# Zero-filled full-row subtraction product, halves of 288 queries, and earlier maxima in the first batch of an attention and two-MLP kernel

## The chip, the cores and the metric

The kernel runs on one core of a Trainium2 chip. The metric is the time of one execution on the device in microseconds, from the median of repeated runs. A profiled execution has its own time, beside the span from the first to the last instruction in its trace. TensorE multiplies matrices into PSUM, VectorE, ScalarE (ACT) and GpSimd (POOL) work on elements, and the SyncE queue (SP) issues the DMAs.

## The reference

The inputs are `q`, `k` and `v` of 4 batches, 8 heads, 576 positions and 64 dimensions. Scores below the row's maximum less `tau` are dropped before the softmax. The heads' outputs are put side by side to 2304 rows of 512 and go through two MLPs with 2048 hidden columns; the first applies a rational function, the second a clipped square.

```python
scores = scale * np.matmul(q, k.transpose(0, 1, 3, 2))
thresh = np.max(scores, axis=-1, keepdims=True) - tau
scores = np.where(scores >= thresh, scores, -1000000000.0)
attn = np.exp(scores - np.max(scores, axis=-1, keepdims=True))
attn = attn / (np.sum(attn, axis=-1, keepdims=True) + 1e-09)
out = np.matmul(attn, v)
# first MLP
h = x @ w_in
P = a[0] + a[1] * h + a[2] * h2 + a[3] * h3
Q = 1.0 + np.abs(b[0]) * np.abs(h) + np.abs(b[1]) * h2
x = (P / (Q + 1e-06)) @ w_out
# second MLP
h = x @ w_in
x = np.where(h >= 1, h, np.where(h <= -1, 0.0, (h + 1) ** 2 / 4)) @ w_out
```

## The kernel before

The heads of a batch are taken in four pairs (`NP`). A head's 576 positions (`S`) are four tiles of 128 and a tail of 64; the tails of both heads of a pair share one tile, so a pair has nine tiles of columns in the transposed queries and keys `qkT`: four of the first head, the shared tail, four of the second. Queries and keys are split into two 16-bit halves; `kT2` holds the keys with their halves exchanged, so that two products make one score tile.

The first batch is handled apart from the others. Before it there is nothing to lay its work beside, except the first MLP's weights: these come as 64-bit floats, and are converted by VectorE (lines 222 to 224), ACT (240, 211, 202) and POOL (206), while the first batch runs. For each pair, `row_max` (line 495) computes the scores with queries in rows, into one PSUM bank at a time, and reduces each to the row's maximum (`most`, line 508). The maxima are cut into three 16-bit pieces (lines 533 to 537), and a product with the identity lays them into three rows of queries, `mrow` (lines 538 to 543). `transposed` (line 546) then computes the scores with keys in rows: for each tile two score products and a third that subtracts the maximum, with `less16` (three rows with the negated weights of the pieces) as weights and `mrow` as the moving operand (line 560). The 576 queries of a tile go as 512 and 64 columns, since a bank holds 512. ACT takes the exponential (562), VectorE drops what is below the threshold (563), and `sums` (566) multiplies the result by the values in 32 bits, again 512 and 64 columns, into two banks that add up over all tiles of a head. `take` (574) copies a finished head's sums to SBUF, `divide` (581) divides by them.

`first_attention` (597) sets the order. It walks nine tiles for each pair; `held` keeps the sums one tile behind the scores. `row_max` is a generator of three pieces: the maxima of the first head, those of the second, and the rest with `mrow`. The next pair's pieces are called for at steps 1, 4 and 7 of a pair (`n % 3 == 1`), and the pair after that is prepared (`prep_pair`, line 311: six loads, scaling, splitting, a transposing DMA and two copies into `kT2`) at step 4. `qkT` and `kT2` have two buffers each. The calls give priorities; the order in which each engine's instructions stand is worked out by a planner from priorities and its own estimate of times, and each engine then runs its list in order.

After the first batch, 192 steps of the two MLPs follow, with the conversion of the second MLP's weights and the attention of the other three batches laid beside them.

Of the kernel before, what the change touches and what calls it, by code (L numbers as in the profile page):

```python
# [9 lines left out]
F16 = mybir.dt.float16  # L10
F32 = mybir.dt.float32
# [20 lines left out]
N_TEMP, N_POLY, N_WT, N_WH, N_GG, N_ROW, N_SC = 5, 3, 3, 2, 4, 3, 2  # L32
# [7 lines left out]
def tile_attention_moe_moe2(  # L40
# [18 lines left out]
    V, A, G, T, Q = nc.vector, nc.scalar, nc.gpsimd, nc.tensor, nc.sync  # L59
    B, H, S, D = q.shape  # L60
    P = 128
    NP = H // 2
    NT = S // P
    ST = S - NT * P
    C = 2 * NT + 1
# [9 lines left out]
    W = NF * TB  # L75
# [5 lines left out]
    ap = ctx.enter_context(tc.tile_pool(name="ap", bufs=2))  # L81
    xp = ctx.enter_context(tc.tile_pool(name="xp", bufs=1))
    mp = ctx.enter_context(tc.tile_pool(name="mp", bufs=2))
    sp = ctx.enter_context(tc.tile_pool(name="sp", bufs=4))
    dp = ctx.enter_context(tc.tile_pool(name="dp", bufs=1, space=DRAM))
    ps_1 = ctx.enter_context(tc.tile_pool(name="ps_1", bufs=1, space=PSUM))
    ps_2 = ctx.enter_context(tc.tile_pool(name="ps_2", bufs=1, space=PSUM))
# [2 lines left out]
    ident = cp.tile([P, P], F32, name="ident")  # L90
    make_identity(nc, ident)
    fixed = mp.tile([P, 2 * W], F16, name="fixed", tag="gg", bufs=N_GG)
    ident16, less16 = fixed[:, 0:P], fixed[0:3, P : 2 * P]
    V.tensor_copy(ident16, ident)
    less = cp.tile([3, 1], F32, name="less")
    V.tensor_scalar(less, ident[0:3, 0:1], -PIECES[0], None, op0=ALU.mult)
    for n in range(1, 3):
        V.scalar_tensor_tensor(less, ident[0:3, n : n + 1], -PIECES[n], less, op0=ALU.mult, op1=ALU.add)
    V.tensor_copy(less16, less.to_broadcast([3, P]))


    def small(n, name, keep=False):
# [246 lines left out]
    M = NT * P  # L349
# [145 lines left out]
    def row_max(pr, qkT, kT2):  # L495
        k1 = qkT[:, C:, :].rearrange("p c s -> p (c s)")
        k2 = kT2.rearrange("p c s -> p (c s)")
        mx = sp.tile([P, 18], F32, name=f"mx0_{pr}", tag="c2", bufs=3)

        def bank(name):  # L500
            return ps_1.tile([P, 512], F32, name=f"sm{pr}_{name}", tag="ph0")

        def dots(dst, c, cols, k0):
            n = dst.shape[-1]
            T.matmul(dst, qkT[:, c, cols], k1[:, k0 : k0 + n], start=True, stop=False)
            T.matmul(dst, qkT[:, c, cols], k2[:, k0 : k0 + n], start=False, stop=True)

        def most(n, src, m=1):
            V.tensor_reduce(mx[:, n : n + m], src, axis=AX.X, op=ALU.max)

        halves = [slice(i * ST, (i + 1) * ST) for i in range(2)]
        for ab in range(2):
            for t in range(NT):
                s = bank(f"{ab}{t}")
                dots(s, ab * (NT + 1) + t, slice(0, P), ab * (M + P))
                most(ab * NT + t, s)
            yield
        s = bank("t").rearrange("p (n k) -> p n k", n=2 * NT)
        for n in range(2 * NT):
            dots(s[:, n], n + n // NT, slice(0, P), M + n // NT * ST)  # L520
        most(2 * NT + 1, s, 2 * NT)
        s = bank("r")
        for i, r in enumerate(halves):
            dots(s[r], NT, r, i * (M + P))
        most(2 * NT, s)
        s = bank("rt")[:, 0:ST]
        for i, r in enumerate(halves):
            dots(s[r], NT, r, M + i * ST)
        most(4 * NT + 1, s)
        n = 2 * NT + 1  # L530
        m = mx[:, 0:n]
        V.tensor_tensor(m, m, mx[:, n:], op=ALU.max)
        pcs = sp.tile([P, 3, n], F16, name=f"pcs{pr}", tag="ka", bufs=2)
        for x in range(3):
            V.tensor_scalar(pcs[:, x], m, 1.0 / PIECES[x], None, op0=ALU.mult)
            if x < 2:
                V.scalar_tensor_tensor(m, pcs[:, x], -PIECES[x], m, op0=ALU.mult, op1=ALU.add)
        mrow = ap.tile([P, 2 * S], F16, name=f"mrow{pr}", tag="hl", bufs=N_ROW)[0:3]
        for c0, c1 in ((0, NT), (NT, 2 * NT), (2 * NT, n)):
            pm = ps_1.tile([P, 512], F32, name=f"pmr{pr}_{c0}", tag="aux")  # L540
            for c in range(c0, c1):
                T.matmul(pm[0:3, (c - c0) * P : (c - c0 + 1) * P], pcs[:, :, c], ident16, start=True, stop=True)
            A.copy(mrow[:, c0 * P : c1 * P], pm[0:3, 0 : (c1 - c0) * P])
        yield mrow

    def transposed(pr, ab, t, data, n):

        con, qkT, kT2, mrow = data
        name = f"{pr}_{ab}_{t}"
        s = ps_2.tile([P, 1024], F32, name="st" + name, tag="acc" if n % 2 else "s")[:, 0:S]  # L550
        q1 = qkT[:, 0:C, :].rearrange("p c s -> p (c s)")
        tiles = [(ab, slice(0, P), slice(0, P), ab * (NT + 1) + t)]
        if t == NT:
            tiles = [(i, slice(i * ST, (i + 1) * ST), slice(i * ST, (i + 1) * ST), NT) for i in range(2)]
        for i, r, cols, c in tiles:
            for to, k0, m0, w in ((0, i * (M + P), i * M, M), (M, M + i * ST, 2 * M + i * ST, ST)):
                dst = s[r, to : to + w]
                T.matmul(dst, qkT[:, C + c, cols], q1[:, k0 : k0 + w], start=True, stop=False)
                T.matmul(dst, kT2[:, c, cols], q1[:, k0 : k0 + w], start=False, stop=False)
                T.matmul(dst, less16[:, 0 : r.stop - r.start], mrow[:, m0 : m0 + w], start=False, stop=True)  # L560
        e = mp.tile([P, 2 * W], F32, name="et" + name, tag="tp", bufs=N_TEMP)[:, 0:S]
        A.activation(e, s, AF.Exp, scale=con[:, 0:1])
        V.scalar_tensor_tensor(e, s, con[:, 2:3], e, op0=ALU.is_ge, op1=ALU.mult)
        return e

    def sums(pv, ab, pr, t, e, vv, first, last):

        w = vv[pr][:, t, ab : ab + 2] if t < NT else vv[NP][:, pr, ab : ab + 2]
        w = w.rearrange("p x d -> p (x d)")
        r = slice(ab * ST, (ab + 1) * ST) if t == NT else slice(0, P)  # L570
        for dst, c0 in pv:
            T.matmul(dst, w[r], e[r, c0 : c0 + dst.shape[-1]], start=first, stop=last)

    def take(pv, ab, x, d):
        h, o = (slice(i * D, (i + 1) * D) for i in (ab, 1 - ab))
        for src, c0 in pv:
            c = slice(c0, c0 + src.shape[-1])
            A.copy(d[h, c], src[o])
            A.copy(x[h, c], src[h])

    def divide(pr, x, d):
        r = mp.tile([P, 2 * W], F32, name=f"rd0_{pr}", tag="tp", bufs=N_TEMP)[:, 0:S]
# [14 lines left out]
    def first_attention():  # L597

        ahead = [prep_pair(0, 0, False)]
        yield  # L600
        vv = first_v()
        yield
        xT[0] = [xp.tile([P, 2 * KT, TB], F16, name=f"xT0_{j}", tag="xT", bufs=NB) for j in range(NB)]
        ahead.append(prep_pair(0, 1, False))
        yield
        for mrow in row_max(0, *ahead[0][1:]):
            yield
        n = 0
        for pr in range(NP):
            con, qkT, kT2 = ahead.pop(0)  # L610
            data = con, qkT, kT2, mrow
            rows = row_max(pr + 1, *ahead[0][1:]) if ahead else iter(())
            x = ap.tile([P, S], F32, name=f"x0_{pr}", tag="e", bufs=N_SC)
            d = ap.tile([P, S], F32, name=f"d0_{pr}", tag="sc", bufs=N_SC)
            held = []
            for ab, t in [(0, t) for t in range(NT + 1)] + [(1, t) for t in range(NT)]:
                e = transposed(pr, ab, t, data, n)
                for f in held:
                    f()
                if t == 0:  # L620
                    pv = [(ps_1.tile([P, 512], F32, name=f"pv0_{pr}_{ab}", tag="pv"), 0),
                          (ps_1.tile([P, 512], F32, name=f"pt0_{pr}_{ab}", tag="ph1")[:, 0:ST], M)]
                    held = [partial(sums, pv, 1, pr, NT, tail, vv, True, False)] if ab else []
                    held.append(partial(sums, pv, ab, pr, t, e, vv, not ab, False))
                elif t == NT or (ab and t == NT - 1):
                    held = [partial(sums, pv, ab, pr, t, e, vv, False, True), partial(take, pv, ab, x, d)]
                    tail = e
                else:
                    held = [partial(sums, pv, ab, pr, t, e, vv, False, False)]
                if n % 3 == 1:  # L630
                    mrow = next(rows, None)
                if n % 9 == 4 and pr + 2 < NP:
                    ahead.append(prep_pair(0, pr + 2, False))
                n += 1
                yield
            for f in held:
                f()
            divide(pr, x, d)
        yield
# [201 lines left out]
    for n in range(N_FIRST):  # L841
        with at(36 * n / N_FIRST - 40):
            next(att)
        while halves and len(halves) * N_FIRST > 2 * NCH * (N_FIRST - 1 - n):
            with at(2.4 * (2 * NCH - len(halves)) - 40):
                i, x = halves.pop(0)
# [83 lines left out]
```

## Time and profile before

| | us |
|---|---|
| median of 3 runs | 1297.07 |
| lowest and highest of the 3 | 1291.64, 1303.17 |
| the profiled execution's own time | 1302.64 |
| its span | 1300.5 |
| busy in the span: TensorE products | 1121.9 |
| VectorE | 1015.2 |
| ACT | 823.8 |
| POOL | 499.4 |

Busy shares are means over the whole span, whose stages differ; the first batch lies in about the first 224 us of it. Starts of TensorE's products are recorded, their ends are modelled, so that products that follow each other seem to overlap: what one costs is read from start to start. The clock column gives what TensorE was granted of its 2.4 GHz; its lower level is 1.2 GHz, 0.5 in these columns.

### The profile page before, as it was taken

The numbers are of one execution on the slowest core, as the hardware profiler recorded it, in microseconds if no ns is written. First come the engines' busy times: TensorE is split into PE (matmuls) and PEld (weight loads), VectorE is DVE, ScalarE is ACT, GpSimd is POOL, SyncE is SP. The second block draws the span as 40 slices with busy tenths as digits, with TensorE's granted clock in tenths as the row PEclk, the third lists the DMA queues.
The fourth block names the chain that finished last, engine by engine and source line by source line (L and its number), as shares of the span: only waits on it lengthen the run. The fifth ranks groups of instructions, "written<-read, shape, count | busy, mean of one in ns | idle before, by whom it ended". The sixth has DMA issues, their size and how long they took to land.

```text
span 1300.5 us, 31124 instructions
## 1 busy us (share of the span) xinstructions
PE 1121.9 (86%) x12354; PEld 973.5 (75%) x12354; DVE 1015.2 (78%) x2399; ACT 823.8 (63%) x1469; POOL 499.4 (38%) x673
## 2 busy tenths in 40 slices
PE   2689779478784889999889999999789998999998
PEld 1244334378683778889878899898778998999998
DVE  6687654999999887768999776889997677897431
ACT  3466454676766667757777577777765766676332
POOL 2223211553553555531146355422454554122221
PEclk9699677598986999989999999999899999999999
DMA  7644431633377567771379465901794559106100
GB/s 207 197 148 157 143 130 69 234 119 131 131 281 238 116 114 129 146 216 44 87 183 219 88 124 139 245 34 44 182 220 88 105 102 266 46 2 208 53 14 25
DMA packets 220273, 176.34 MB, mean 136 GB/s; under 512 B 181984, under 2 KB 193248, under 8 KB 211936
## 3 DMA queue, kind: packets, MB, share of 16 engines
q1 hardware_dynamic: 220128, 174.36, 50.3%
q8 instruction: 96, 1.57, 0.5%
q14 instruction: 49, 0.40, 0.1%
HBM read 106.83 MB, written 21.50 MB: 99 GB/s over the span
## 4 chain that ended last, share of the span: by engine, by line
PE 33%; DVE 21%; DMA 8%; issue 5%; POOL 4%; ACT 3%; SPq 1%; DVEq 0%; ACTq 0%; POOLq 0%
PE acc L829 14%; PE ph L815 14%; DMA eT<-hl 5%; DVE e L373 2%; PE pv L399 2%; POOL hl L384 2%; DVE sc L411 2%; DVE t L708 2%; DVE t L707 2%; DVE t L709 1%; DVE t L702 1%; DMA rqk<-in_k_dram 1%; DVE t L703 1%; DVE t L704 1%; DVE qk L209 1%
## 5 line engine op out<-in xcount | busy, mean ns | idle before, releaser
L829 PE MATMUL acc<-gg,wc 128*128 128x192 f16 x4608 | 432.7, 249 | 26.8 <-POOL gg L206 12.6
L815 PEld LDWEIGHTS <-wc 128*128 128x128 f16 x4608 | 393.6, 100 | 28.4 <-issue 15.4
L829 PEld LDWEIGHTS <-wc 128*128 128x128 f16 x4608 | 389.1, 99 | 28.8 <-issue 26.8
L206 POOL TENSOR_TENSOR gg<-t,gg 128x384 f16<-128x384 f32 x192 | 190.1, 992 | 447.2 <-ACT gg L202 370.0
L815 PE MATMUL ph<-xT,wc 128*128 128x192 f16 x2304 | 221.1, 254 | 16.5 <-DVE t L704 11.5
L815 PE MATMUL ph<-yT,wc 128*128 128x192 f16 x2304 | 218.8, 249 | 3.3 <-DVE t L762 2.4
L384 POOL TENSOR_TENSOR hl<-e,hl 128x256 f16<-128x256 f32 x216 | 156.1, 744 | 0.0
L202 ACT CAST gg<-t 128x384 f16<-128x384 f32 x192 | 96.9, 507 | 71.0 <-DVE t L762 33.1
L761 DVE SCALAR_TENSOR_TENSOR t<-t,c 128x384 f32<-128x384 f32 x96 | 64.8, 675 | 70.9 <-ACT t L760 70.8
L373 DVE SCALAR_TENSOR_TENSOR e<-sc,nt,e 128x576 f32<-128x576 f32 x108 | 93.3, 865 | 31.8 <-ACT e L372 31.1
L206 POOL TENSOR_TENSOR wc<-wt,wc 128x256 f16<-128x256 f32 x64 | 46.7, 763 | 143.3 <-ACT wc L202 143.3
L372 ACT ACTIVATE e<-sc,nt,con 128x576 f32<-128x576 f32 x108 | 93.5, 866 | 10.6 <-POOL hl L384 3.7
L760 ACT ACTIVATE t<-ph,c 128x384 f32<-128x384 f32 x96 | 64.0, 667 | 50.6 <-PE ph L815 50.3
L399 PE MATMUL pv<-v,eT 128*128 128x65 f16 (+3 forms) x1680 | 71.7, 196 | 23.5 <-DMA eT<-hl 23.3
L381 ACT CAST hl<-e 128x576 f16<-128x576 f32 x108 | 72.2, 668 | 30.0 <-DVE e L373 29.2
L700 ACT ACTIVATE t<-ph,sc 128x384 f32<-128x384 f32 x96 | 55.4, 577 | 54.9 <-PE ph L815 54.8
L399 PEld LDWEIGHTS <-eT 128*128 128x128 f16 (+1 forms) x1680 | 64.4, 102 | 32.6 <-DMA eT<-hl 29.4
L382 POOL TENSOR_TENSOR hl<-e,hl 128x64 f16<-128x64 f32 x108 | 39.4, 365 | 128.2 <-ACT hl L381 125.8
L411 DVE TENSOR_SCALAR_CACHE_REDUCE sc<-s 128x576 f32<-128x576 f32 x108 | 80.8, 748 | 9.4 <-PE s L366 8.9
L705 ACT ACTIVATE t<-t,lc 128x384 f32<-128x384 f32 x96 | 67.9, 707 | 18.3 <-DVE t L702 18.0
L365 PE MATMUL s<-qkT 128*128 128x512 f16 (+1 forms) x240 | 64.3, 295 | 14.7 <-DVE sc L411 12.1
L412 ACT ACTIVATE nt<-mx,ln_e,con 128x1 f32<-128x1 f32 x108 | 41.6, 385 | 54.3 <-DVE sc L411 53.7
(218 smaller groups left out, 1891.8 us busy)
## 6 DMA issues: line engine op xcount, KB each, us to landing
wc<-scratch SPq DMA_DIRECT2D x56, 1024.0 KB, 5.7
rw<-in_moe_w_in_dram SPq DMA_DIRECT2D x16, 1024.0 KB, 5.4
rw<-in_moe_w_out_dram SPq DMA_DIRECT2D x16, 1024.0 KB, 5.1
scratch<-wc SPq DMA_DIRECT2D x8, 1024.0 KB, 4.0
scratch<-wh SPq DMA_DIRECT2D x16, 512.0 KB, 2.8
kT<-qkT SPq DMA_DIRECT2D x32, 144.0 KB, 2.4
rqk<-in_q_dram SPq DMA_DIRECT2D x16, 256.0 KB, 3.1
rqk<-in_k_dram SPq DMA_DIRECT2D x16, 256.0 KB, 3.0
```

The source lines that it names most:

```text
L202: A.copy(hi, src)
L206: G.tensor_tensor(lo[:, p], src[:, p], hi[:, p], op=ALU.subtract)
L372: A.activation(e, s, AF.Exp, bias=nb, scale=con[:, 0:1])
L373: V.scalar_tensor_tensor(e, s, th, e, op0=ALU.is_ge, op1=ALU.mult)
L381: A.copy(hi, e)
L384: G.tensor_tensor(lo_w[:, p], e[:, whole][:, p], hi[:, whole][:, p], op=ALU.subtract)
L399: T.matmul(pv[rows, 0:w], eT[:, c, cols], vv[:, h * NT + x if x < NT else H * NT + h, at : at + w], start=(n == 0), stop=(n == len(blocks) ...
L411: V.tensor_scalar(s, banks[:, 0:S], 1.0, -LARGEST, op0=ALU.mult, op1=ALU.max, accum_out=mx)
L705: A.activation(r, u, AF.Ln, bias=lc[:, 1:2], scale=lc[:, 0:1])
L761: V.scalar_tensor_tensor(u, u, top, u, op0=ALU.min, op1=ALU.mult)
L815: last = T.matmul(ph[:, f, :], w[:, wx, kt, f * P : (f + 1) * P], rhs, start=(n == 0), stop=(n == 3 * KT - 1))
L829: T.matmul(dst, w[:, wx, f, d * P : (d + 1) * P], gg[:, gx, f, :], start=(i == 0 and f == 0 and n == 0 and d % 2 == 0), stop=(i == NCH - 1 ...
```

## The change

The subtraction's weights get 128 rows, with zeros from row 3 on, and `mrow` becomes a tile of 128 rows that POOL fills with zeros before ACT writes the first three. The maxima are numbered in the order of the columns of `qkT` (first head, tail, second head), so that the queries of a head are one run of 576 columns; it is cut into two halves of 288, each in a bank of its own, for the scores and for the sums. `take` copies the halves; for the second head, whose tail comes first, the second half of `take` has three pieces. The reduction of the eight tail products is made in two. The three pieces of the next pair's maxima are called for at steps 0, 2 and 4 of a pair, the preparation of the pair after that at step 5.

```diff
@@ -90,13 +90,14 @@
     ident = cp.tile([P, P], F32, name="ident")
     make_identity(nc, ident)
     fixed = mp.tile([P, 2 * W], F16, name="fixed", tag="gg", bufs=N_GG)
-    ident16, less16 = fixed[:, 0:P], fixed[0:3, P : 2 * P]
+    ident16, less16 = fixed[:, 0:P], fixed[:, P : 2 * P]
     V.tensor_copy(ident16, ident)
     less = cp.tile([3, 1], F32, name="less")
     V.tensor_scalar(less, ident[0:3, 0:1], -PIECES[0], None, op0=ALU.mult)
     for n in range(1, 3):
         V.scalar_tensor_tensor(less, ident[0:3, n : n + 1], -PIECES[n], less, op0=ALU.mult, op1=ALU.add)
-    V.tensor_copy(less16, less.to_broadcast([3, P]))
+    G.memset(less16, 0.0)
+    V.tensor_copy(less16[0:3], less.to_broadcast([3, P]))
 
 
     def small(n, name, keep=False):
@@ -513,20 +514,21 @@
             for t in range(NT):
                 s = bank(f"{ab}{t}")
                 dots(s, ab * (NT + 1) + t, slice(0, P), ab * (M + P))
-                most(ab * NT + t, s)
+                most(ab * (NT + 1) + t, s)
             yield
         s = bank("t").rearrange("p (n k) -> p n k", n=2 * NT)
         for n in range(2 * NT):
             dots(s[:, n], n + n // NT, slice(0, P), M + n // NT * ST)
-        most(2 * NT + 1, s, 2 * NT)
+        for ab in range(2):
+            most(2 * NT + 1 + ab * (NT + 1), s[:, ab * NT : (ab + 1) * NT], NT)
         s = bank("r")
         for i, r in enumerate(halves):
             dots(s[r], NT, r, i * (M + P))
-        most(2 * NT, s)
+        most(NT, s)
         s = bank("rt")[:, 0:ST]
         for i, r in enumerate(halves):
             dots(s[r], NT, r, M + i * ST)
-        most(4 * NT + 1, s)
+        most(3 * NT + 1, s)
         n = 2 * NT + 1
         m = mx[:, 0:n]
         V.tensor_tensor(m, m, mx[:, n:], op=ALU.max)
@@ -535,30 +537,32 @@
             V.tensor_scalar(pcs[:, x], m, 1.0 / PIECES[x], None, op0=ALU.mult)
             if x < 2:
                 V.scalar_tensor_tensor(m, pcs[:, x], -PIECES[x], m, op0=ALU.mult, op1=ALU.add)
-        mrow = ap.tile([P, 2 * S], F16, name=f"mrow{pr}", tag="hl", bufs=N_ROW)[0:3]
+        mrow = ap.tile([P, 2 * S], F16, name=f"mrow{pr}", tag="hl", bufs=N_ROW)
+        G.memset(mrow, 0.0)
         for c0, c1 in ((0, NT), (NT, 2 * NT), (2 * NT, n)):
             pm = ps_1.tile([P, 512], F32, name=f"pmr{pr}_{c0}", tag="aux")
             for c in range(c0, c1):
                 T.matmul(pm[0:3, (c - c0) * P : (c - c0 + 1) * P], pcs[:, :, c], ident16, start=True, stop=True)
-            A.copy(mrow[:, c0 * P : c1 * P], pm[0:3, 0 : (c1 - c0) * P])
+            A.copy(mrow[0:3, c0 * P : c1 * P], pm[0:3, 0 : (c1 - c0) * P])
         yield mrow
 
     def transposed(pr, ab, t, data, n):
 
         con, qkT, kT2, mrow = data
         name = f"{pr}_{ab}_{t}"
-        s = ps_2.tile([P, 1024], F32, name="st" + name, tag="acc" if n % 2 else "s")[:, 0:S]
+        s = ps_2.tile([P, 1024], F32, name="st" + name, tag="acc" if n % 2 else "s")
+        s = s.rearrange("p (z n) -> p z n", z=2)[:, :, 0 : S // 2]
         q1 = qkT[:, 0:C, :].rearrange("p c s -> p (c s)")
         tiles = [(ab, slice(0, P), slice(0, P), ab * (NT + 1) + t)]
         if t == NT:
             tiles = [(i, slice(i * ST, (i + 1) * ST), slice(i * ST, (i + 1) * ST), NT) for i in range(2)]
         for i, r, cols, c in tiles:
-            for to, k0, m0, w in ((0, i * (M + P), i * M, M), (M, M + i * ST, 2 * M + i * ST, ST)):
-                dst = s[r, to : to + w]
-                T.matmul(dst, qkT[:, C + c, cols], q1[:, k0 : k0 + w], start=True, stop=False)
-                T.matmul(dst, kT2[:, c, cols], q1[:, k0 : k0 + w], start=False, stop=False)
-                T.matmul(dst, less16[:, 0 : r.stop - r.start], mrow[:, m0 : m0 + w], start=False, stop=True)
-        e = mp.tile([P, 2 * W], F32, name="et" + name, tag="tp", bufs=N_TEMP)[:, 0:S]
+            for z in range(2):
+                dst, of = s[r, z], slice(i * S + z * S // 2, i * S + (z + 1) * S // 2)
+                T.matmul(dst, qkT[:, C + c, cols], q1[:, of], start=True, stop=False)
+                T.matmul(dst, kT2[:, c, cols], q1[:, of], start=False, stop=False)
+                T.matmul(dst, less16[:, 0 : r.stop - r.start], mrow[:, of], start=False, stop=True)
+        e = mp.tile([P, 2 * W], F32, name="et" + name, tag="tp", bufs=N_TEMP)[:, 0:S].rearrange("p (z n) -> p z n", z=2)
         A.activation(e, s, AF.Exp, scale=con[:, 0:1])
         V.scalar_tensor_tensor(e, s, con[:, 2:3], e, op0=ALU.is_ge, op1=ALU.mult)
         return e
@@ -568,15 +572,16 @@
         w = vv[pr][:, t, ab : ab + 2] if t < NT else vv[NP][:, pr, ab : ab + 2]
         w = w.rearrange("p x d -> p (x d)")
         r = slice(ab * ST, (ab + 1) * ST) if t == NT else slice(0, P)
-        for dst, c0 in pv:
-            T.matmul(dst, w[r], e[r, c0 : c0 + dst.shape[-1]], start=first, stop=last)
+        for z in range(2):
+            T.matmul(pv[z], w[r], e[r, z], start=first, stop=last)
 
     def take(pv, ab, x, d):
         h, o = (slice(i * D, (i + 1) * D) for i in (ab, 1 - ab))
-        for src, c0 in pv:
-            c = slice(c0, c0 + src.shape[-1])
-            A.copy(d[h, c], src[o])
-            A.copy(x[h, c], src[h])
+        half = S // 2
+        for src, c0, c1, to in ((0, 0, ST, M), (0, ST, half, 0), (1, 0, half, half - ST)) if ab else ((0, 0, half, 0), (1, 0, half, half)):
+            c = slice(to, to + c1 - c0)
+            A.copy(d[h, c], pv[src][o, c0:c1])
+            A.copy(x[h, c], pv[src][h, c0:c1])
 
     def divide(pr, x, d):
         r = mp.tile([P, 2 * W], F32, name=f"rd0_{pr}", tag="tp", bufs=N_TEMP)[:, 0:S]
@@ -618,8 +623,8 @@
                 for f in held:
                     f()
                 if t == 0:
-                    pv = [(ps_1.tile([P, 512], F32, name=f"pv0_{pr}_{ab}", tag="pv"), 0),
-                          (ps_1.tile([P, 512], F32, name=f"pt0_{pr}_{ab}", tag="ph1")[:, 0:ST], M)]
+                    pv = [ps_1.tile([P, 512], F32, name=f"pv{z}_{pr}_{ab}", tag=tag)[:, 0 : S // 2]
+                          for z, tag in enumerate(("pv", "ph1"))]
                     held = [partial(sums, pv, 1, pr, NT, tail, vv, True, False)] if ab else []
                     held.append(partial(sums, pv, ab, pr, t, e, vv, not ab, False))
                 elif t == NT or (ab and t == NT - 1):
@@ -627,9 +632,9 @@
                     tail = e
                 else:
                     held = [partial(sums, pv, ab, pr, t, e, vv, False, False)]
-                if n % 3 == 1:
+                if n % 9 in (0, 2, 4):
                     mrow = next(rows, None)
-                if n % 9 == 4 and pr + 2 < NP:
+                if n % 9 == 5 and pr + 2 < NP:
                     ahead.append(prep_pair(0, pr + 2, False))
                 n += 1
                 yield
```

## Rows read from the trace of the kernel before

**Rows 1.** Busy time of each engine by stretch of the first batch, then granted clock and DMA.

```profile
core 0: us, PE busy (x) PEld busy (x) DVE busy (x) ACT busy (x) POOL busy (x), PEclk, DMA share, GB/s
60.50:88.20 27.70, 27.20 (x144) 13.71 (x144) 20.33 (x40) 16.95 (x26) 11.91 (x14) 0.96 0.31 98
88.20:100.80 12.60, 8.62 (x35) 3.16 (x33) 10.98 (x26) 9.73 (x21) 0.18 (x1) 0.72 0.76 237
100.80:129.70 28.90, 27.64 (x138) 13.39 (x138) 20.75 (x43) 19.29 (x28) 11.95 (x15) 0.95 0.39 142
129.70:143.20 13.50, 6.50 (x33) 3.13 (x31) 12.34 (x22) 8.71 (x18) 3.60 (x4) 0.68 0.71 197
143.20:174.50 31.30, 31.22 (x117) 13.92 (x117) 19.01 (x35) 15.86 (x25) 5.73 (x10) 0.81 0.37 135
174.50:190.00 15.50, 7.35 (x52) 4.14 (x51) 9.72 (x23) 6.70 (x14) 2.10 (x5) 0.64 0.37 136
190.00:223.50 33.50, 33.46 (x110) 14.79 (x110) 12.53 (x28) 14.47 (x22) 7.62 (x12) 0.66 0.17 63
223.50:330.00 106.50, 71.88 (x672) 66.75 (x672) 99.59 (x195) 76.12 (x124) 48.20 (x50) 0.79 0.45 154
```

**Rows 2.** TensorE's timeline, one step at full clock: start, time, line.

```profile
165.50 1.12 PE L572 MATMUL pv<-et,v 128*128 128x512 f32 x2
166.46 0.33 PE L572 MATMUL pt<-et,v 128*128 128x64 f32 x2
166.63 0.38 PE L558 MATMUL st<-qkT 128*128 128x512 f16 x1
166.85 0.38 PE L559 MATMUL st<-qkT,kT 128*128 128x512 f16 x1
167.16 0.39 PE L560 MATMUL st<-mrow,fixed 3*128 3x512 f16 x1
167.48 0.20 PE L558 MATMUL st<-qkT 128*128 128x64 f16 x1
...
167.77 1.12 PE L572 MATMUL pv<-et,v 128*128 128x512 f32 x2
```

**Rows 3.** The same timeline, sums behind a product with all its rows.

```profile
170.26 0.38 PE L506 MATMUL sm<-kT,qkT 128*128 128x512 f16 x1
170.48 1.02 PE L572 MATMUL pv<-et,v 128*128 128x512 f32 x2
171.34 0.33 PE L572 MATMUL pt<-et,v 128*128 128x64 f32 x2
```

**Rows 4.** The same timeline, first products of two steps at the lower clock.

```profile
192.21 0.63 PE L558 MATMUL st<-qkT 128*128 128x512 f16 x1
...
196.31 0.63 PE L558 MATMUL st<-qkT 128*128 128x512 f16 x1
```

**Rows 5.** The same timeline around the first maxima and two turns of pairs.

```profile
29.11 0.61 PE L506 MATMUL sm<-kT,qkT 128*128 128x512 f16 x1 [1.58 <-DMA kT<-qkT]
...
57.69 0.28 PE L560 MATMUL st<-mrow,fixed 3*128 3x64 f16 x2
...
83.15 0.38 PE L559 MATMUL st<-qkT,kT 128*128 128x512 f16 x1
...
91.85 0.39 PE L506 MATMUL sm<-kT,qkT 128*128 128x512 f16 x1 [2.61 <-DMA kT<-qkT]
...
135.13 0.59 PE L542 MATMUL pmr<-fixed,pcs 128*3 128x128 f16 x4 [4.58 <-DVE pcs L535]
```

**Rows 6.** Groups of instructions from 0 to 340 us.

```profile
L563 DVE SCALAR_TENSOR_TENSOR et<-st,con,et 128x576 f32<-128x576 f32 x36 | 29.1, 812 | 18.4 <-ACT et L562 18.2
...
L578 ACT COPY d<-pv 64x512 f32<-64x512 f32 x8 | 4.6, 580 | 3.8 <-PE pv L572 3.6
...
L476 POOL MEMSET v<- 128x256 f32 x5 | 1.3, 315 | 0.0
```

**Rows 7.** Waits from 25 to 230 us: total, times, longest.

```profile
POOL wc L206 <- ACT wc L202: 131.5, 8, 18.8
```

## The prediction

> **What bounds the kernel now.** The chain of waits that ended last can be followed back only to 315 us, so I read the first batch from other views: busy time by stretch first, then TensorE's own timeline, then the groups of instructions, then the waits. I cut the first batch at the first sum of each pair of heads (60.5, 100.8, 143.2, 190.0) and at the last score tile before each turn to the next pair [rows 1]. Two kinds of stretch come out. Inside a pair TensorE is the bound: busy 27.20 of 27.70, 27.64 of 28.90, 31.22 of 31.30 and 33.46 of 33.50 us. At the three turns (12.6, 13.5 and 15.5 us) it is busy only 8.62, 6.50 and 7.35 us, so 19.1 of 41.6 us are idle, and the granted clock is 0.72, 0.68 and 0.64. The slow clock reaches on into the pair behind: 0.81 in the third and 0.66 in the fourth, though TensorE hardly rests there. From 223.5 to 330 us VectorE is busy 99.59 of 106.5 us: there it is the bound, by work that this change doesn't touch, so what the first batch saves should arrive at the end undiminished.
>
> Inside a pair, one step is two sums of the tile before and six score products [rows 2]. Its starts tell the cost, since ends are modelled: a step runs from 165.50 to 167.77, 2.27 us. A full-row product of 512 columns is followed after 0.22 us (166.63 to 166.85). The one before the three-row product is followed after 0.31, and the three-row product itself after 0.32 (167.16 to 167.48). So each passage into and out of three rows costs about 0.10 us that no column fills.
>
> At a turn the order is: last scores of the pair, then the product that brings the maxima into a row, then the first scores' subtraction. TensorE waited 4.58 us for VectorE's pieces of the maxima, until 135.13 [rows 5]; the next sums come at 143.2 [rows 1]. That chain, maxima of the next pair to their row, is what the turn waits for.
>
> **The change part by part.**
>
> Full rows and two halves. The six products of one group take 167.77 - 166.63 = 1.14 us. Their 1728 columns at 0.22 us per 512 are 0.74. Four passages go, worth 0.40. The long sum that follows a three-row product lasts 0.96 (165.50 to 166.46); after a full-row product it lasts 0.86 (170.48 to 171.34) [rows 2, 3]; this 0.10 goes as well. The sums' 576 columns themselves stay. I take 0.50 to 0.55 us a group, 0.52. In a slow stretch a step is 196.31 - 192.21 = 4.10 us [rows 4], against twice 0.74 plus twice 1.03 (0.86 and the short sum's 0.17) = 3.54, so 0.56. There are 36 score tiles, and the four tail tiles are two groups each: 40 groups, 21 us off TensorE's queue. Only what lies on the path counts, which is all of it in the last pair and little of it where the maxima set the pace.
>
> The rows show that a three-row product doesn't run beside its neighbours: what follows starts 0.32 us later, not earlier. [...]
>
> Maxima earlier. The calls that make the next pair's maxima move from steps 1, 4 and 7 of a pair to 0, 2 and 4. The row of maxima is then due in the middle of the pair, with four steps (some 8 us) to spare. What is late next is the maxima's own chain. It can't begin before the second half of the keys has landed, which needs the buffer that the pair before has just left: from that pair's last key product at 83.15 to the first maximum product at 91.85 are 8.7 us. From there the only chain not spread over a pair is the first one, 29.11 to 57.69, 28.6 us, with VectorE and TensorE passing one bank to and fro and the weight conversion between [rows 5]. So a pair can't be shorter than about 37.3 us, though TensorE needs less: its busy time in the first period is 27.20 + 8.62, less ten groups' 5.2, 30.6 us. The periods now are 40.3, 42.4 and 46.8 [rows 1]; they lose 3.0, 5.1 and 9.5, together 17.6 us. If, as may be, the first chain was stretched by its slow clock and 33 is enough, they lose 7.3, 9.4 and 13.8, 30.5 us.
>
> The last pair has no maxima to make and is bound by TensorE alone. Its 33.5 us at a clock of 0.66 are 22.1 us of full clock. Less 10 x 0.52 they are 16.9: 25.6 us at 0.66 (7.9 saved), 20.9 at 0.81 (12.6 saved), 17.6 at 0.96 (15.9 saved). With a shorter stall before it I take the clock of the third pair, 0.81: 12.6.
>
> Preparing the next pair moves from step 4 to 5. With it six loads of queries and keys, the transposing DMA and two copies of keys go one step later on SP, among the weight loads, and its scaling one step later on ACT, VectorE and POOL. Bound: nothing, if the buffer is what the transfer waits for, to one step of 2.27 us in each of the two pairs that have it. I take 1 each, 2 us lost.
>
> Small things. The row tile is zeroed by POOL four times (1152 half-words; a fill of 256 words took 0.315 us, so 0.3 to 1.4 us each), free as long as it runs before the maxima are ready. The copies of the sums are four of 288 columns for one head and six for the other, where a copy of 512 took 0.580 [rows 6]: two more copies in each of four pairs, 0 to 0.58 us each, on ACT, which has room at the turns. One reduction becomes two of half the length. The pieces at the start (a fill and a copy) lie beside the first loads. I charge 2 us for all of it. Nothing excludes a small gain here either, as the halves let the exponential's input sit evenly in two banks; I count none.
>
> Sum: 17.6 + 12.6 - 2 - 2 = 26 us. The profiled execution took 1302.64 (span 1300.5), so one like it would take 1276.6. It lies 5.6 above the median of the three timed runs, 1297.07, and the forecast is made against that median: 1271.
>
> **The rivals.** First, the calls move but the instructions don't. Each engine's order comes from a planner that places what it believes ready, and the maxima may stay where they were, held by the keys' arrival. Then each pair still ends in a stall; what the steps save is waited away at the turn, and the last pair's 7.9 with a little of the others remains: about 10 us, 1287. For it: the 2.61 us for which the first maximum product waited for the keys [rows 5], which an earlier call can't shorten. Against it: the 4.58 us wait was for pieces of maxima, not for keys.
>
> Second, VectorE becomes the bound. It is busy 93.1 us between 60.5 and 190 [rows 1], and waited only 18.4 us there for the exponential, over the whole first batch [rows 6]. In 3 x 37.3 = 112 us that is 83%. It reaches 94% later [rows 1], but with a long queue of independent work; if 78% is all it can do here, the periods sum to 119, 10 us saved in place of 17.6, 19 in all: 1278.
>
> Third, the clock stays up once the stalls and the empty passages are gone, and the chain is short: 30.5 + 15.9 - 4 = 42, so 1255. For it: after the stretch at 0.96 the turn alone fell to 0.72. Against it: in the last pair 33.46 of 33.5 busy us got only 0.66.
>
> Fourth, the other side: POOL. It works in order, and its weight subtractions stood 131.5 us in eight waits for ACT's casts, up to 18.8 each [rows 7]. If the fill of the row of maxima is queued behind one of these, ACT's copy of the row waits, behind it on ACT the exponentials, and so TensorE. Up to the 8 us of spare steps cost nothing; from about 14.5 in each of the four rows of maxima the gain is gone, and at 18.8 in each 4 x 10.8 = 43 us are lost: 1297 - 26 + 43 = 1314. Against it: POOL is far from full, and a planner sees the fill ready early.
>
> Fifth, the three-row products do run beside their neighbours in some place that I haven't read: then the last pair gains no 12.6 but pays for the columns of its ten subtractions, 576 at 0.22 per 512 or 0.25 each, 2.5; 17.6 - 2.5 - 4 = 11 are saved: 1286. The 0.32 us of [rows 2] speak against it. [...]
>
> **How the numbers follow.** Forecast 0.50 (1260 to 1282), clock up 0.10, VectorE 0.12, calls without effect 0.18, POOL 0.08, overlap 0.02. A measurement of this kernel tells about 1%, 13 us, from no change: the runs lie between 1291.64 and 1303.17. Faster by more is the forecast, the clock, VectorE and a little of the first rival (0.04): 0.76. Within it are the rest of the first rival, the overlap and a mild case of POOL: 0.17. Slower: 0.07. The range of 1252 to 1290 holds the forecast, VectorE, most of the first rival and half of the clock; it leaves out POOL and the ends, under 0.2.
>
> **What would show it.** In the profile after: products of 288 columns about 0.12 us apart at full clock, with no 0.10 us gaps around the subtraction; a step of some 1.75 us; the product that makes the row of maxima in the middle of a pair, and no wait of several us for it; turns without idle TensorE, or with a wait for the keys in place of that for the maxima; the first batch's last sum at about 197 us where it is at 223; the granted clock of the last pair above 0.66. The prediction is wrong if the first sums of the pairs still lie over 40 us apart, if ACT's copy of the row waits for POOL, or if the stretch after the first batch grows by what the batch lost.

## The result, and the profile after

The changed kernel takes 1310.41 us (median of 8 runs, 1304.95 to 1313.71), against 1296.18 (8 runs, 1291.64 to 1303.17) for the kernel before in the same comparison: ratio 1.0104, 95% interval 1.0075 to 1.0133. It is slower by 1%; the forecast was 1271, and the range ended at 1290.

Busy time by stretch in the changed kernel, cut at the first sum of each pair and at the last sum of the batch as in [rows 1], then three stretches behind the batch:

```profile
core 0: us, PE busy (x) PEld busy (x) DVE busy (x) ACT busy (x) POOL busy (x), PEclk, DMA share, GB/s
61.50:89.80 28.30, 24.30 (x152) 15.08 (x152) 21.06 (x40) 17.97 (x32) 6.10 (x9) 1.00 0.28 101
89.80:148.70 58.90, 39.03 (x180) 21.59 (x180) 38.67 (x76) 31.28 (x55) 15.39 (x18) 0.68 0.42 138
148.70:195.90 47.20, 32.99 (x183) 20.03 (x183) 31.48 (x66) 25.75 (x44) 10.79 (x15) 0.78 0.39 121
195.90:217.30 21.40, 19.76 (x102) 13.21 (x102) 14.91 (x32) 15.25 (x23) 6.64 (x8) 0.92 0.38 135
217.30:330.00 112.70, 80.61 (x778) 75.33 (x777) 100.85 (x198) 80.28 (x135) 57.01 (x58) 0.82 0.39 138
330.00:380.00 50.00, 40.13 (x429) 38.30 (x427) 45.56 (x85) 33.64 (x56) 22.16 (x22) 0.93 0.61 222
380.00:440.00 60.00, 18.14 (x101) 12.32 (x99) 49.43 (x148) 29.92 (x50) 24.80 (x35) 0.56 0.69 201
```

The first and the last pair are shorter (28.3 and 21.4 us, turns included; before 40.3 and 33.5), but the second is 58.9 where it was 42.4, and the third is 47.2 where it was 46.8. The batch still ends 5.9 us earlier, at 217.3. Then TensorE has little to do from 380 to 440 us: it is busy 18.14 of 60, where the kernel before has 40.39 in the same stretch:

```profile
380.00:440.00 60.00, 40.39 (x391) 34.37 (x389) 55.59 (x174) 37.95 (x66) 28.75 (x39) 0.80 0.69 212
```

So there are two surprises, one in the batch and one behind it.

TensorE's timeline after: one step of a pair, then the users of one PSUM bank over two rows of maxima.

```profile
63.79 1.13 PE L576 MATMUL pv<-et,v 128*128 128x288 f32 x4
64.76 0.29 PE L562 MATMUL st<-qkT 128*128 128x288 f16 x1
64.88 0.29 PE L563 MATMUL st<-qkT,kT 128*128 128x288 f16 x1
65.00 0.29 PE L564 MATMUL st<-mrow,fixed 128*128 128x288 f16 x1
65.12 0.29 PE L562 MATMUL st<-qkT 128*128 128x288 f16 x1
65.25 0.29 PE L563 MATMUL st<-qkT,kT 128*128 128x288 f16 x1
65.37 0.29 PE L564 MATMUL st<-mrow,fixed 128*128 128x288 f16 x1
65.49 0.38 PE L506 MATMUL sm<-qkT 128*128 128x512 f16 x1
...
87.34 0.22 PE L545 MATMUL pmr<-fixed,pcs 128*3 128x128 f16 x1 [0.75 <-ACT mrow L546]
88.16 0.49 PE L182 MATMUL pmmw<-ident,mb 128*128 128x128 f32 x2 [0.26 <-ACT mrow L546]
94.95 0.61 PE L251 MATMUL pg<-wc 128*128 128x128 f16 x8
99.13 0.71 PE L182 MATMUL pmmqke<-ident,mqk 128*128 128x128 f32 x4
101.39 0.38 PE L182 MATMUL pmmw<-ident,mb 128*128 128x128 f32 x2
...
143.04 0.59 PE L545 MATMUL pmr<-fixed,pcs 128*3 128x128 f16 x4 [1.56 <-DVE pcs L537]
146.36 0.27 PE L545 MATMUL pmr<-fixed,pcs 128*3 128x128 f16 x1
147.01 1.15 PE L182 MATMUL pmmqke<-ident,mqk 128*128 128x128 f32 x4
150.48 0.38 PE L182 MATMUL pmmw<-ident,mb 128*128 128x128 f32 x2
```

The step is as forecast: six products 0.12 us apart, 1.70 from the sums to the next group [rows 2: 2.27]. Below it, `pmr` lays the maxima into a row, `pmmqke` finds the bound by which a pair's queries and keys are scaled (the start of `prep_pair`), `pmmw` that of half a weight chunk, and `pg` is the norm of a chunk. All four take their tile from one bank of PSUM, `aux`, with one buffer:

```python
place = ps_1.tile([P, 512], F32, name="pm" + name, tag="aux")       # everywhere()
pm = ps_1.tile([P, 512], F32, name=f"pmr{pr}_{c0}", tag="aux")      # row_max()
```

In the trace these users keep the order of the calls. Before, the preparation of pair 2 (counted from 0) was called at step 4 and the row of pair 1 at step 7; now the row is called at step 4 and the preparation at 5. So the preparation of pair 2 runs at 99.13, behind the row, and that of pair 3 at 147.01, right behind the row of pair 2. In the kernel before they ran at

```profile
73.57 0.61 PE L181 MATMUL pmmqke<-ident,mqk 128*128 128x128 f32 x4
...
117.14 0.71 PE L181 MATMUL pmmqke<-ident,mqk 128*128 128x128 f32 x4
```

The row of pair 1 has left the bank at 88.11; a half's bound (88.16) and its norm (94.95) come before the preparation of pair 2 as well. That of pair 3 waits for nothing but ACT's last copy of the row, as its weight load (PEld) shows:

```profile
146.97 0.93 PEld L182 LDWEIGHTS pmmqke<-ident,mqk 128*128 128x128 f32 x4 [0.28 <-ACT mrow L546]
```

Row, preparation, transposing DMA (113.0), keys (landed 120.0), maxima, row (143.04 to 146.36): the chain of a pair begins only when the row of the pair before is made.

### The profile page after: what moved, and what is told of

The parts are those of the page before. It is cut to its first block, busy times and chain, and to the rows that moved or that the text cites. A ratio compares the mean times of both kernels' runs of the same rounds, so it can differ in the third digit from the quotient of the medians.

```text
span 1309.2 us, 31145 instructions
## 1 busy us (share of the span) xinstructions
PE 1096.2 (84%) x12354; PEld 977.9 (75%) x12354; DVE 1022.1 (78%) x2403; ACT 823.1 (63%) x1477; POOL 504.7 (39%) x678
## 4 chain that ended last, share of the span: by engine, by line
PE 36%; DVE 15%; DMA 10%; issue 3%; POOL 3%; ACT 2%; SPq 1%; DVEq 0%; ACTq 0%; POOLq 0%
PE acc L834 15%; PE ph L820 15%; DMA eT<-hl 6%; PE pv L400 2%; DVE e L374 2%; POOL hl L385 2%; DMA qkT<-qk 2%; DVE sc L412 1%; DVE t L713 1%; DVE t L712 1%; PE s L367 1%; PE s L366 1%; DVE qk L210 1%; DMA rqk<-in_k_dram 1%; DVE t L714 1%
## 5 line engine op out<-in xcount | busy, mean ns | idle before, releaser
L712 DVE SCALAR_TENSOR_TENSOR t<-t,ka,t 128x384 f32<-128x384 f32 x96 | 65.8, 686 | 14.7 <-ACT t L711 14.0
```

The costliest lines, as they stand in the source:

```text
L712: V.scalar_tensor_tensor(s, s, ka[:, 0:1], r, op0=ALU.add, op1=ALU.mult)
```

## The experiments

Each is one edit. Times of one group were compared with runs of the kernel before of that group (medians 1304.08 for the runs e, 1294.72 for f, 1300.41 for g and bare, 1306.85 for h), so kernels of different groups are compared by their ratios. The trace columns, in us: start of the last sum of the first batch; product for the bound of half 16, the first of the second MLP's sixteen half chunks; end of the split of half 31, the last; first product of the second MLP's third step.

| kernel | median | ratio, 95% interval | last sum | half 16 | half 31 | third step |
|---|---|---|---|---|---|---|
| before | 1296.18 | | 223.2 | 229 | 405.9 | 417.6 |
| after | 1310.41 | 1.0104 (1.0075, 1.0133) | 217.3 | 231 | 421.8 | 437.0 |
| e_calls | 1332.91 | 1.0204 (1.0155, 1.0253) | 254.7 | 261 | 443.8 | 455.1 |
| e_product | 1282.36 | 0.9841 (0.9802, 0.9880) | 202.6 | 213 | 390.6 | 400.8 |
| e_prep4 | 1297.99 | 0.9959 (0.9929, 0.9989) | 211.4 | 230 | 413.7 | 419.0 |
| e_prep3 | 1293.23 | 0.9904 (0.9871, 0.9937) | 199.1 | 213 | 403.9 | 419.7 |
| f_rows | 1299.61 | 1.0007 (0.9963, 1.0051) | 205.5 | 213 | 402.8 | 414.7 |
| f_halves | 1304.95 | 1.0038 (0.9990, 1.0087) | 230.1 | 237 | 415.0 | 422.1 |
| f_bank | 1271.95 | 0.9816 (0.9773, 0.9858) | 222.0 | 181 | 369.2 | 401.5 |
| g_before_bank | 1282.64 | 0.9838 (0.9762, 0.9914) | 244.4 | 181 | 353.4 | 407.9 |
| g_product_bank | 1277.56 | 0.9795 (0.9712, 0.9879) | 228.0 | 180 | 374.5 | 401.4 |
| h_both_bank | 1279.27 | 0.9805 (0.9739, 0.9871) | 252.1 | 164 | 342.9 | 408.1 |
| bare_before | 1235.88 | 0.9486 (0.9379, 0.9592) | 214.3 | | | 355.2 |
| bare_after | 1250.50 | 0.9598 (0.9513, 0.9682) | 220.4 | | | 383.6 |

**The change taken apart.** e_product is the changed kernel with the calls as before; e_calls is the kernel before with the calls as after.

```diff
-                if n % 9 in (0, 2, 4):
+                if n % 3 == 1:
                     mrow = next(rows, None)
-                if n % 9 == 5 and pr + 2 < NP:
+                if n % 9 == 4 and pr + 2 < NP:
```

> The full rows, the halves of 288 and the new copies alone; the maxima are called for at steps 1, 4, 7 and the preparation at step 4, as before. Theory A (the order of calls is at fault: the preparation of the pair after next takes the one bank that it shares with the row of maxima, and the bank is handed out in the order of the calls): the preparation's product comes in the first pair's middle, the pairs' first sums lie 36 to 42 us apart, the first batch's last sum comes at 203 to 215 us (223 before, 217 in the changed kernel), and the time is 1280 to 1295. Theory B (faster products let the tiles run ahead and leave the maxima bare): as the changed kernel, a period near 58 us in the second pair, time 1303 to 1313.

> The moved calls alone (maxima at steps 0, 2, 4, preparation at 5), with the products of before. Theory A: the preparation's product waits until the row of maxima has left the shared bank, the second pair's period is 50 to 60 us, the time is 1303 to 1325. Theory B: the maxima come earlier and nothing is lost, 1285 to 1297.

Measured 1282.36 and 1332.91: the product is worth 1.6%, the earlier calls cost 2.0% alone. In e_calls the preparations come at 109.9 and 158.2, behind the rows. So theory A has the order right, but not every size: in e_calls the second period is 66.6 us, not 50 to 60, and the time lies above its range; in e_product the second period is 44.8, over 42, and the last sum, at 202.6, just ahead of its range.

**Where the preparation is called.** e_prep4 and e_prep3 are the changed kernel with `n % 9 == 4` and `n % 9 == 3` for the preparation; at 4 it is still called behind the row's piece, at 3 ahead of it.

> The changed kernel with the preparation back at step 4, but behind the call for the third piece of maxima in that step. Theory A: the order in which the bank is handed out is the same, so the time is that of the changed kernel, 1303 to 1315, and the preparation's product still follows the row of maxima. Rival (one step later is what costs): 1275 to 1295.

> The changed kernel with the preparation at step 3, ahead of the third piece of maxima. Theory A: the preparation's product comes in the middle of the first pair, no period is over 45 us, the last sum is at 190 to 207 us and the time 1270 to 1292. Theory B: no better than the changed kernel, 1303 to 1313. If the last sum comes early but the time stays over 1300, the loss is made behind the first batch, in the conversion of the second MLP's weights.

Measured 1297.99 and 1293.23. At 4 the preparation of pair 2 runs at 88.8, directly behind the row, ahead of the half's bound and norm that stand between the two in the changed kernel. So one step of the call is worth about 10 us at this place. The ratio falls from 1.0104 to 0.9959, and both ranges are missed: theory A had taken the order for unchanged. At 3 the preparations come at 74.2 and 114.0, the second pair takes 44.9 us in place of 58.9, and the batch ends at 199.1, as forecast; the time lies just above its range. Only 1% arrives: 24 us are gained in the batch, some 12 at the end.

**The parts of the product.** f_rows is the kernel before with 128 rows for `less16` and `mrow` alone, f_halves with 288 + 288 columns alone, still with three rows.

```diff
-    ident16, less16 = fixed[:, 0:P], fixed[0:3, P : 2 * P]
+    ident16, less16 = fixed[:, 0:P], fixed[:, P : 2 * P]
...
+        G.memset(mrow, 0.0)
```

> The subtraction with 128 rows alone; 512 and 64 columns, calls and copies as before. If the passages into and out of three rows are the gain, 40 groups lose 0.50 us each on TensorE, 20 us, and most of the gain of full rows and halves together is here: 1280 to 1292. If the halves bring it: 1294 to 1306, as before.

> The halves of 288 with the subtraction still in three rows; calls as before. The four passages of a group stay, so by the passages it is the kernel before, 1292 to 1308. If the halves bring the gain: 1280 to 1290.

TensorE's timelines of f_rows and then of f_halves, the latter at the lower clock:

```profile
62.29 0.38 PE L560 MATMUL st<-qkT 128*128 128x512 f16 x1
62.50 0.38 PE L561 MATMUL st<-qkT,kT 128*128 128x512 f16 x1
62.72 0.38 PE L562 MATMUL st<-mrow,fixed 128*128 128x512 f16 x1
62.94 0.19 PE L560 MATMUL st<-qkT 128*128 128x64 f16 x1
62.96 0.19 PE L561 MATMUL st<-qkT,kT 128*128 128x64 f16 x1
```

```profile
63.74 0.45 PE L560 MATMUL st<-qkT 128*128 128x288 f16 x1
63.98 0.45 PE L561 MATMUL st<-qkT,kT 128*128 128x288 f16 x1
64.36 0.42 PE L562 MATMUL st<-mrow,fixed 3*128 3x288 f16 x1
64.71 0.42 PE L560 MATMUL st<-qkT 128*128 128x288 f16 x1
```

With 128 rows the 512-column products follow each other after 0.22 us, the subtraction included (0.31 and 0.32 in [rows 2]). With three rows of 288 columns the steps into and out of the subtraction are 0.38 and 0.35 here, 0.24 between the two others; at full clock the median steps are 0.22 each, against 0.12 in the changed kernel. So a passage costs 0.10 us with 512 columns and with 288, and the rows remove it, not the halves. f_rows ends the batch 17.7 us earlier than before (205.5), so most of the 20 us are there, and takes the same time (1299.61), above the range that went with them; f_halves ends it 7 us later and takes the same time, too. Neither part alone brings the 1.6% of e_product; why both together do is not shown.

**The bank.** In f_bank the row of the changed kernel takes its three tiles from `ph0`, the bank in which the maxima are computed; g_before_bank is that one edit in the kernel before, g_product_bank in e_product.

```diff
-            pm = ps_1.tile([P, 512], F32, name=f"pmr{pr}_{c0}", tag="aux")
+            pm = ps_1.tile([P, 512], F32, name=f"pmr{pr}_{c0}", tag="ph0")
```

> The changed kernel, calls as they are, but the row of maxima is made in the bank of the maxima's scores and no longer in the one that the preparation uses. Theory A (order in the shared bank): the preparation for the third pair no longer waits for the row of maxima, its product comes before 85 us, no period of the pairs is over 45 us, the first batch's last sum is at or before 207 us and the time 1275 to 1297. Rival (the later call itself, or the planner): the preparation's product stays at 90 to 100 us and the time at 1303 to 1315.

> The kernel before with one edit: the three tiles of the row of maxima (pmr) come from the PSUM bank ph0, in which that pair's maxima are taken, and no longer from aux, through which every half of a weight and every preparation also finds its bound. Bank theory: the row holds up not only the preparation but the weight conversions; off aux they run ahead, the last half of the second MLP is split by 370 to 395 (before 405.9) and the time falls to 1265 to 1285. Rival, the bank matters only where the preparation is called behind the row, which is the changed kernel alone: 1290 to 1302, within 1% of the kernel before.

> Full-row product, halves of 288 and copies as in the changed kernel, the calls as before (1, 4, 7 and 4), and the row's tiles in ph0. Bank theory: the weight conversions gain here too: last half split by 360 to 385 (390.6 with the tiles in aux), time 1255 to 1278. Rival, the gain of the product (1282) and the gain of the bank in the changed kernel (1272) are the same 20 us, set by something behind the first batch: 1270 to 1284, and the conversion's end tells nothing.

All three take 1272 to 1283, 1.6 to 2% less than the kernel before, one of them without any part of the change. Their batches end at 222.0, 244.4 and 228.0, hardly earlier than before (223.2) or later. What is earlier is the weights: half 16 gets its bound at 180 or 181, the last half is split at 353 to 375. Intervals of the three overlap; f_bank has the lowest median and beats both kernels.

In f_bank theory A is right about the preparation, which comes at 65.4, and wrong about the batch: the first period is 48.3 us and the last sum comes at 222.0, not by 207, so the gain is not the one it had in mind. The time of g_product_bank lies in both of its ranges and tells nothing between them.

Four of these kernels make a square. With the row in `aux` the moved calls turn 0.9841 (e_product) into 1.0104 (the changed kernel); with the row in `ph0` they turn 0.9795 (g_product_bank) into 0.9816 (f_bank), and these intervals overlap. So the moved calls cost time only where the row is in `aux`. With the row in `ph0` the product, too, is worth little: 0.9838 (g_before_bank) against 0.9795, with overlapping intervals.

**The weights freed, the preparation not.** h_both_bank is f_bank with `pmmqke` of the first batch in `ph0`, too, behind the row.

```diff
+            s = root(..., everywhere(f"mqke{b}_{pr}", mx, 2, place=ps_1.tile([P, 512], F32, name=f"pmmqke{b}_{pr}", tag="ph0")), 2)
```

> The changed kernel with the row's tiles in ph0 and the first batch's preparation (pmmqke) in ph0 behind them: the preparation of a pair still waits for the row of the pair before, as in the changed kernel, but the weights' bounds have aux for themselves. If the row's hold on the weights is the larger part, the last half of the second MLP is split by 365 to 390 (421.8 in the changed kernel) and the time is 1272 to 1290 though the preparation of pair 2 comes at 90 or later. Rival, the preparation behind the row is the larger part: 1295 to 1312.

Its TensorE timeline, the weights' half 8 and the preparation of pair 2 behind the row:

```profile
80.00 0.49 PE L182 MATMUL pmmw<-ident,mb 128*128 128x128 f32 x2
...
113.58 0.27 PE L545 MATMUL pmr<-fixed,pcs 128*3 128x128 f16 x1
114.23 1.18 PE L182 MATMUL pmmqke<-ident,mqk 128*128 128x128 f32 x4
```

The preparations run at 114.2 and 171.3, later than in the changed kernel, and the batch ends at 252.1, the second latest of all. But half 8 has its bound at 80.0, 1.2 us after ACT's pass over it, where it came at 150.48 in the changed kernel, 30 us after that pass (119.96) and behind row and preparation. The last half is split at 342.9, earlier than said, and the time is 1279.27, ratio 0.9805. So the late preparation lengthens the batch, but by itself it costs no time at the end. TensorE from 380 to 440 us, same columns as above:

```profile
380.00:440.00 60.00, 57.31 (x695) 54.69 (x693) 54.73 (x142) 35.38 (x68) 26.57 (x35) 0.95 0.74 213
```

**Without the second MLP's conversion.** bare_before and bare_after leave out the conversion of the second MLP's sixteen half chunks and load the first MLP's in their place, so they don't compute the same function:

```diff
-    spread(*WEIGHTS, [("w", i, x) for i in range(NCH) for x in range(2)])
+    f_w[1] = f_w[0]
+    f_max[1] = [f_max[0][1], f_max[0][1]]
...
-        Q.dma_start(wc, scratch[m][i])
+        Q.dma_start(wc, scratch[0][i])
```

> The kernel before without the conversion of the second MLP's weights (the bounds of the first MLP's are used, and its halves are loaded again from DRAM in their place; these 32 halves are left out). It is the base for the next run. If that conversion holds the second MLP back, the time falls by 25 to 60 us below the kernel before, and the first product of step 32 comes before 420 (before: 451.9). If not, it falls by under 15.

> The changed kernel with the same left out. Theory: behind the first batch the time is lost only through the second MLP's conversion, so without it the difference between the two kernels is that of the last sums of the first batch (217.3 against 223.2), 3 to 9 us in favour of the changed kernel. Rival: the changed kernel also lost its time elsewhere (the steps of the MLP or the second batch); then it stays 8 to 16 us slower than the kernel before with the same left out.

Measured 1235.88 and 1250.50. The second MLP no longer waits for its weights: from its second step to its third are 4.4 us in both, against 33.7 before and 62.4 after. What bare_before saves (64.5 us by the medians, a little over its range) is not this wait alone, since the conversion's own work on the engines is left out, too. The second expectation fell: the batch ends later in bare_after than in bare_before (220.4 against 214.3; why is not shown), and the medians differ by 14.6 us, inside the range of the rival, by which the changed kernel loses time elsewhere as well. For the rival: the second MLP's third step comes 28.4 us later (383.6 against 355.2), and from 260 to 380 us VectorE is busy all 120 us, 109.30 in bare_before. Against it: the spans of the two traces differ by 5.9 only (1243.6 and 1237.7), and the intervals of the ratios overlap. So the pair shows the wait for the weights; whether the changed kernel also loses in the steps of the first MLP stays open.

## Why the prediction was wrong

**The step that failed first: the preparation.** "Bound: nothing ... to one step of 2.27 us in each of the two pairs" measured 25.6 us for pair 2 and 29.9 for pair 3. I had followed SP's queue and the engines' lists, but not what the instruction writes to. The bank `aux` is a queue as much as an engine is, and moving the row's call ahead of the preparation's turned the order of two of its users round. The second period came to 58.9 and the third to 47.2, where 37.3 was the forecast; the wait "for pieces of maxima" that I meant to take away was replaced by a longer loop. In the terms of the sum: the turns were to save 17.6 us, and the three periods together grew by 4.9 (129.5 to 134.4). The Trainium skill (Perfetto Trace Analysis, Optimization Strategy) says that a gap which repeats on an engine can mean that there is no PSUM for the next tile; here the trace agrees: TensorE is idle 19.9 of 58.9 and 14.2 of 47.2 us in these periods, and with the row's tiles in another bank the preparation comes at 65.4. The bank itself shows only as waits of 0.26 and 0.28 us for ACT's copy of the row (`pmmw` at 88.16, `pmmqke` at 146.97), because its users already stand in this order in TensorE's list.

**The step that failed second: the gain arrives "at the end undiminished".** It doesn't, in either direction. f_rows and e_prep3 end the batch 17.7 and 24.1 us earlier than before and take 0 and 1% less; h_both_bank ends it 28.9 later and takes 2% less. What the time follows is when the second MLP's weights are converted. VectorE's timeline in the changed kernel shows the gate, the one result that all of the second MLP waits for (first line: the maximum over the bounds of all halves):

```profile
413.64 0.14 DVE L255 TENSOR_REDUCE f_max<-f_w 128x1 f32<-128x8 f32 x1
...
419.35 0.57 DVE L728 TENSOR_SCALAR sr<-sr 128x8 f32<-128x8 f32 x1
...
422.82 0.16 DVE L732 TENSOR_TENSOR w2b<-w2b,sr 128x8 f32<-128x8 f32 x1
...
427.21 0.15 DVE L753 TENSOR_TENSOR c<-c 128x8 f32<-128x8 f32 x1
```

and ACT's and TensorE's what waits for it:

```profile
428.09 1.22 ACT L765 ACTIVATE t<-ph,c 128x384 f32<-128x384 f32 x2
```

```profile
374.62 1.56 PE L820 MATMUL ph<-yT,wc 128*128 128x192 f16 x17 [0.82 <-DVE t L709]
...
436.24 0.94 PE L400 MATMUL pv<-v,eT 128*128 128x65 f16 x14 [3.74 <-DMA eT<-hl]
436.99 1.31 PE L820 MATMUL ph<-yT,wc 128*128 128x192 f16 x7
```

No clipped square of the second MLP can be taken before the last half's bound is in `f_max`; two steps fill both banks `ph` at 371 and 374.62, and the third starts at 436.99. The first MLP's steps had come earlier (the last one starts at 365.7, before 379.1): that gain was waited away. From e_product to e_calls the last half is split 53.2 us later (390.6, 443.8) and the time is 50.6 longer. Below about 375 this ends: the four kernels split at 342.9 to 374.5 have ratios of 0.9795 to 0.9838 in another order; in h_both_bank VectorE is busy 50.00 of the 50 us from 330 to 380 and is the bound there.

One thing that puts the conversion late is shown: the bounds of all halves go through `aux`, so each row of maxima holds them up, and off `aux` they run ahead. By the moved calls half 16 comes 17 us later than in e_product (231 against 213). The rest is not explained. Against the kernel before, half 16 is only 2 us late, and the other 14 us come behind it, where VectorE's list is laid out by the planner: when the first pass over half 24 starts, 9 steps of the first MLP have begun on VectorE before, 13 after, none in the four kernels with the row in `ph0`. But f_rows has 9 as well and needs 190 us from half 16 to half 31, where the kernel before needs 176, so this count isn't the cause alone. What sets this stretch (172 to 194 us in these kernels) stays open; it was not tried.

**What was right.** The passage of 0.10 us, shown by f_rows and f_halves; the step, 1.70 where 1.75 was said; the last pair, 21.4 where 20.9 was said. This one is in part luck: the 20.9 went with a clock of 0.81, and at the 0.92 that was granted the same sum, 16.9 us of full clock, gives 18.4. The small things: POOL's fills take 1.06 us each, four of them; three stand before 5 us and one at 81.3, and none delays a row, so the fourth rival, the one that forecast a slower kernel, was not what made it slow. The bound of 37.3 us for a period was wrong, too: the first took 28.3.

**The rivals.** Calls without effect: false, they had a large one. VectorE as bound inside the batch: not there, 38.67 of 58.9 us. Clock up: true of the last pair, of no use. Overlap of three-row products: false, as their starts show. The Trainium skill (TensorEngine Tiling (Array Packing), Key Properties) says that changing the tiling mode drains TensorE; if three rows count as a mode of their own, the 0.10 us are its price here, though no run shows the drain itself.

Taken together: the product saves (e_product, -1.6%), and the earlier calls cost more than that, but only while the row of maxima is in `aux` (1.0104; 0.9816 with the row in `ph0`). The bank's order explains the long periods of the batch; the time is lost behind the batch, at the second MLP's weights, and not by the late preparation itself (h_both_bank). The row's hold on `aux` costs the kernel before as much as the product saves.

## What to carry to other kernels

List the users of every buffer that has only one copy, with their order, as you list an engine's queue: a call that moves past another user of the same bank takes its place, and what the other user feeds moves by a whole loop and not by a step. Before a gain in one stage is carried to the end, look for the latest of all that the next stage waits for; here it was a conversion in the background, and one tile moved to another bank gained what the whole product did.

## What the runs showed of the hardware

At full clock a product with three rows between products of 128 rows costs 0.10 us on the way in and 0.10 on the way out, with 512 columns and with 288. A pair's granted clock is not told by how busy TensorE is: the last pair of the kernel before got 0.66 at 33.46 of 33.50 us busy [rows 1], that of the changed kernel 0.92 at 19.76 of 21.40, and that of f_rows, whose columns are cut as before, 0.89 at 21.67 of 22.50; g_before_bank, with three rows, got 0.93 at 24.20 of 27.90, so the rows are not what makes the difference, and what does stays open.
